# Scaled states ahead of the squares on ScalarE, the next unit's products behind the states on VectorE, and four weight halves made a unit earlier

## The chip, the cores and the metric

One core of one Trainium2 chip runs the whole program. The metric is the device time of one execution in microseconds; a change is compared by medians of several executions on the same chip.

## What is computed

Two batches of 768 tokens, 8 heads of 48. A recurrent attention with a decay per channel feeds a gated two-matrix layer, and that feeds a spatial gating layer:

```python
for t in range(S):
    cur = einsum('bhd,bhe->bhde', u * k[t], v[t])
    y[t] = einsum('bhd,bhde->bhe', r[t], state + cur)
    state = w[t][..., None] * state + einsum('bhd,bhe->bhde', k[t], v[t])
...
k = maximum(xk @ w_k, 0);  v = (k * k) @ w_v          # 384 -> 1024 -> 384
r = sigmoid(xr @ w_r);     x = r * v                  # 384 -> 384
...
h = gelu(x @ w_in);  u, v = halves of h               # 384 -> 1024
out = x + (u * (w_sg @ norm(v) + b_sg)) @ w_out
```

## The kernel before

The 1536 tokens are cut into four groups of 384 (three chunks of 128). The attention goes by **units**: a unit is one pair of heads in one group, so there are 16, numbered 0 to 15 here (the words "units 9 to 16" of the change are units 8 to 15). TensorE's order is written out by hand as a list of keys: for a unit S (transposes `kt_ps`, the bonus sum `ab`, the scores `sc`), K (the states `kv`), Y (masked scores times v into `y`) and Z (running states times `rp` into `y`), and for a group's first layer `k`, `r` and `v` (`moe1_k`, `moe1_r`, `moe1_v`). The units of group s+1 are spread between the matmuls of group s: units 8 to 11 lie in group 1's `k`, `r` and `v` (84 to 122 us), units 12 to 15 in group 2's (130 to 167 us). From there on TensorE runs the remaining layers without attention.

From group 1 on the `k` and `r` matmuls take each operand in two halves (high and low), three matmuls per product. The low halves are VectorE subtractions: `xkl`, `xrl` of the activations, `wkl`, `wrl`, `wvl` of the weights (`split1`, line 354; the high half `wh` is a ScalarE copy), `kl` of the squared k tile.

What a unit asks of the other engines, in the order of the data:

- `attn_prep` (line 444): VectorE scans `pf` and `pr` of the decays, then `kp` = k times `pr` and `rp` = r times `pf`.
- `rk_make` (line 477): GpSimd makes `ru` = r times k of the next unit, released by VectorE's `ru` product of this one; `bonus_halves` (line 531): ScalarE's `rh` high half and VectorE's `rh` low half of it, which TensorE's two `ab` matmuls read.
- `self_am` (line 540): VectorE masks the scores (`am`, two instructions), which Y reads.
- `attn_kv` (line 553): ScalarE's copy `kt` feeds the `kv` matmuls; VectorE turns them into running states (`zt`, and `zcar` for the group's last); ScalarE scales each into `sblk` or `scar`, two 48x48 instructions a state (line 592), which Z reads.
- `moe1_k` and `moe1_sq` (lines 742 and 755): for each of the eight k tiles ScalarE takes the relu `kr` out of PSUM, squares it into `kh` and then into `kr` itself, and VectorE subtracts them into `kl`. `kr` has two buffers, `mm` in PSUM has three.

On ScalarE and VectorE a scheduler sorts the instructions by a due time (`with at(t)`) where their data allow it; `tc.issue_after(x)` forbids an instruction to be put ahead of x on its engine. It adds order, not a transfer of data. DMAs on SP (SyncE) are sorted the same way. In the kernel before, a k tile's `kl` was held behind the unit's last state, and its squares were held by nothing:

```python
if split_ops[0] and s and (head.get("unit") or 0) > NP and (s, f) not in hold_sq:
    head.setdefault("kl", []).append(low)      # low: the subtraction alone
...
if kd == "K":
    for f in head.pop("kl", []):
        with tc.issue_after(st[g]["zt"]):
            f()
```

The eight `wkl` were made as five behind group 0's last `v` tile (`LO_HEAD = 5`, in `moe1_v`) and three later, from the list `lows`, which `LO_AT` empties behind the states of units 8, 9 and 10 (three, three and four halves).

Of the kernel before, what the change touches and what calls it, by code (L numbers as in the profile page):

```python
# [6 lines left out]
F32 = mybir.dt.float32  # L7
# [37 lines left out]
B_AM = 2  # L45
B_KP = 3
T_START = 7
LO_AT = {8: 3, 9: 3, 10: 4}
LO_LAST = 11
LO_HEAD = 5  # L50
T_GAP = 2.5
T_TAIL = 9.0
VQ = 4
# [19 lines left out]
def emit(tc, tin, nin, vt, consts, ucp, pars, b_sg, w_k, w_v, w_r, w_in, w_sgT, w_out, outT):  # L73
# [479 lines left out]
    def attn_kv(i):  # L553
        tY = TS["Y", i] if i < NP else TS["K", i] + 1.1
        s = st[i]
        hp = i % NP
        g, c0, nc_ = subs[i // NP]
        si = i // NP
        last = g % GB == GB - 1 and c0 + nc_ == CG
        nk = nc_ - 1 if last else nc_  # L560
        kv = pq.tile([128, 512], F32, name="kv", tag="kv", bufs=1)
        kv3 = kv[0:PR, 0:nc_ * D].rearrange("p (c d) -> p c d", d=D)
        for c in range(nk):
            for h in range(2):
                hs = slice(h * HP, HP if h == 0 else PR)
                PE.matmul(kv3[hs, c], s["kt"][:, c, hs], uv[i][:, c, h * D:h * D + D], start=(c == 0), stop=(c == nk - 1),
                          skip_group_check=True)
        zt = pa.tile([PR, max(1, nc_), D], F32, name="zt", tag="zt", bufs=2)
        first = g % GB == 0 and c0 == 0
        us = [None if first else scar[hp]]  # L570
        z = None if first else (zcar[:, (si + 1) % 2, hp, 0:D], zcar[:, (si + 1) % 2, hp, D:D + 1])
        for c in range(nk):
            o = zcar[:, si % 2, hp, 0:D] if c == nc_ - 1 else zt[:, c]
            with at(tY - 0.6 + (3 if c == nc_ - 1 else 0.2 * c)):
                if z is None:
                    s["zt"] = V.tensor_copy(o, kv3[:, c]).ins  # L576
                else:
                    s["zt"] = V.scalar_tensor_tensor(o, z[0], z[1], kv3[:, c], ALU.mult, ALU.add).ins
            z = (o, s["pe"][c])
            sb = scar[hp] if c == nc_ - 1 else sblk[i % 2][c]  # L580

            def scaled(c=c, o=o, sb=sb):
                if c == nc_ - 1:
                    with at(tY + 3):
                        A.activation(zcar[:, si % 2, hp, D:D + 1], s["pe"][c], AF.Copy)
                with at(tY - 0.5 + (3 if c == nc_ - 1 else 0.2 * c)):
                    for h in range(2):
                        hs = slice(h * HP, h * HP + D)
                        if i == NP - 1 and c == nc_ - 2:
                            V.tensor_scalar(sb[hs, hs], o[hs], s["pe"][c][hs], None, ALU.mult)  # L590
                        else:
                            s["sa"] = A.activation(sb[hs, hs], o[hs], AF.Copy, scale=s["pe"][c][hs]).ins  # L592

            if i < NP:
                s.setdefault("late" if c == nc_ - 1 else "soon", []).append(scaled)
            else:
                scaled()
            us.append(sb)
        s["us"] = us
# [142 lines left out]
    def moe1_k(s, f, c=None):  # L742
        nat, nt = is_nat(s, "k"), subs[s][2] * CH
        ps = moe1_part(s, "k", f, c)
        if ps is None:
            return
        kr = pl["w"].tile([128, nt], F32, name="kr", tag="kr", bufs=2)
        with at(TE["k", s, f]):
            m1[s, "ev", f] = A.activation(kr, ps, AF.Relu).ins
        if split_ops[0] and (s, f) in hold_sq:  # L750
            head["sq"] = lambda: moe1_sq(s, f, kr)
        else:
            moe1_sq(s, f, kr)

    def moe1_sq(s, f, kr):
# [13 lines left out]
        with at(dl):  # L769
            A.activation(kh, kr, AF.Square)  # L770
            A.activation(kr, kr, AF.Square)  # L771

        def low():
            with at(dl):
                V.tensor_tensor(kl, kr, kh.bitcast(F32), ALU.subtract)  # L775

        m1[s, "k", f] = (kh, kl)
        if split_ops[0] and s and (head.get("unit") or 0) > NP and (s, f) not in hold_sq:
            head.setdefault("kl", []).append(low)
        else:  # L780
            low()

    def moe1_r(s, j, c=None):
        nt = subs[s][2] * CH
# [8 lines left out]
    def moe1_v(s, j, q):  # L793
# [10 lines left out]
            V.tensor_tensor(x2[g][:, j, c0 * CH:(c0 + n) * CH], ps, m1[s, "r", j], ALU.mult)  # L804
        if s == NAT["r"] - 1 and j == KM - 1 and split_ops[0]:
            with tc.issue_after(st[2 * NP - 1]["ev"]), tc.issue_after(st[2 * NP - 1]["sa"]):
                for f in range(KF):
                    head["khi"] = split1("k", f, TS["k", s + 1, f], V, f >= LO_HEAD)

    m2 = {}  # L810

# [260 lines left out]
    for n, key in enumerate(keys[:n_in]):  # L1072
# [48 lines left out]
        if kd == "K" and 2 * NP <= g and g + 1 < NU and g != 3 * NP - 1:  # L1121
            with tc.issue_after(st[g]["zt"]):
                products(g + 1)
        if kd == "K" and g == 2 * NP:
            split_rv()
        if kd == "K" and g in LO_AT:
# [39 lines left out]
                    head.pop("sq")()  # L1166
        if kd == "K":
            head["unit"] = None
            for f in head.pop("kl", []):
                with tc.issue_after(st[g]["zt"]):  # L1170
                    f()
        if kd == "k" and key[2:] in ((0 if g in (0, NS - 1) else KM - 1,), (0 if g in (0, NS - 1) else KM - 1, KM - 1)) and g != 1:
            moe1_prep(g, 1, [] if g in (0, NS - 1) else [(m1[g, "ev", f],) for f in range(KM)])
        if kd == "v" and g == NS - 2 and key[2:] == (KM - 1, VQ - 1):
# [87 lines left out]
```

## Time and profile before

| | us |
|---|---|
| median of 3 executions | 338.54 (338.32 to 338.86) |
| the profiled execution | 338.41 |
| its span in the profile | 336.6 |
| TensorE busy in it | 326.6 |
| VectorE busy | 239.7 |
| ScalarE busy | 189.1 |
| GpSimd busy | 36.4 |

The profiled execution's own time is 1.8 us over its span, and 0.13 us under the median. Busy time on TensorE is from the start of a matmul to its modelled end, and neighbouring matmuls overlap, so a stretch in which TensorE waits briefly still reads as busy; the waits have to be read from start times. On VectorE and ScalarE too an instruction's length overlaps the next one's start by some 0.1 us where the two do not depend on each other.

### The profile page before, as it was taken

Reading aid. Unit: us, or ns where it says so; the run is one execution under the profiler, and the core shown is the slowest. Engines: PE = TensorE matmul, PEld = TensorE weight load, DVE = VectorE, ACT = ScalarE, POOL = GpSimd, SP = SyncE. Lnnn points to the kernel's source line nnn. Section 1 sums busy time; section 2 is a strip of 40 time slices with the busy share of each in tenths; the row PEclk is TensorE's granted clock in tenths of the full one; section 3 lists DMA queues with packets and bytes.
Section 4 is the critical chain, followed back from the end, with each engine's and each line's share of the span. In section 5 each row is a group of like instructions: output and inputs, shape, how many; then the busy total and the mean of one; then the engine's idle time right before and its main releaser. Section 6 shows DMA issues by size and latency. Waiting matters only on the chain.

```text
span 336.6 us, 5952 instructions
## 1 busy us (share of the span) xinstructions
PE 326.6 (97%) x2139; PEld 286.6 (85%) x2139; DVE 239.7 (71%) x537; ACT 189.1 (56%) x447; POOL 36.4 (11%) x60
## 2 busy tenths in 40 slices
PE   7999999999998999999999999999999999999993
PEld 3785666666897899988999999988999999999992
DVE  6988988678798996988559461797989723545531
ACT  3667995669977645986449973965533215211100
POOL 3210102010111101011022531000000000000000
PEclk9999999999999999999999999999999999999997
DMA  8888963755333423011026225413230010100022
GB/s 218 207 278 298 306 182 82 200 129 132 129 89 87 116 69 125 18 39 35 19 66 193 88 70 168 133 42 84 61 94 10 1 70 2 48 24 0 0 75 78
DMA packets 23878, 34.22 MB, mean 102 GB/s; under 512 B 3440, under 2 KB 18160, under 8 KB 23840
## 3 DMA queue, kind: packets, MB, share of 16 engines
q1 hardware_dynamic: 21696, 31.34, 32.0%
q10 hardware_dynamic: 2144, 2.41, 2.7%
q8 instruction: 19, 0.31, 0.4%
q14 instruction: 19, 0.16, 0.1%
HBM read 29.02 MB, written 2.36 MB: 93 GB/s over the span
## 4 chain that ended last, share of the span: by engine, by line
PE 65%; DVE 11%; issue 11%; DMA 5%; ACT 4%; POOL 2%; SPq 1%; POOLq 0%; ACTq 0%; DVEq 0%
PE mn L671 28%; PE mm L671 27%; DMA stg<-w_v 2%; DVE pf L458 2%; POOL ru L480 2%; PE y L624 2%; PE sc L514 2%; PE y L610 2%; DMA cst<-consts 2%; PE y L613 1%; DVE kl L775 1%; DVE pr L463 1%; DVE am L546 1%; DVE wvl L368 1%; PE mm L690 1%
## 5 line engine op out<-in xcount | busy, mean ns | idle before, releaser
L659 ACT ACTIVATE gah<-gt 128x384 fp32r<-128x384 f32 x16 | 8.4, 526 | 43.8 <-DVE gt L875 43.8
L480 POOL TENSOR_TENSOR ru<-urk 112x384 f32<-112x384 f32 x15 | 16.9, 1125 | 113.1 <-DVE ru L517 66.0
L592 ACT ACTIVATE sblk<-zt,pf 48x48 f32<-48x48 f32 x62 | 20.4, 330 | 7.1 <-DVE zt L576 3.9
L671 PE MATMUL mm<-kh,wh 128*128 128x384 f32 x64 | 22.0, 343 | 0.0
L671 PE MATMUL mm<-kh,wvl 128*128 128x384 f32 x64 | 21.6, 337 | 0.0
L671 PE MATMUL mm<-kl,wh 128*128 128x384 f32 x64 | 21.5, 336 | 0.0
L775 DVE TENSOR_TENSOR kl<-kr,kh 128x384 fp32r<-128x384 f32 x24 | 14.4, 601 | 9.1 <-ACT kr L771 9.1
L671 PE MATMUL mm<-xkh,wh 128*128 128x384 f32 x57 | 20.5, 360 | 0.0
L671 PE MATMUL mn<-wsh,vl 128*128 128x384 f32 x60 | 20.0, 334 | 0.0
L671 PE MATMUL mn<-wsh,vh 128*128 128x384 f32 x60 | 20.0, 334 | 0.0
L671 PE MATMUL mn<-wsl,vh 128*128 128x384 f32 x60 | 20.0, 334 | 0.0
L671 PE MATMUL mm<-xkh,wkl 128*128 128x384 f32 x57 | 19.2, 337 | 0.0
L671 PE MATMUL mm<-xkl,wh 128*128 128x384 f32 x57 | 19.2, 337 | 0.0
L546 DVE TENSOR_TENSOR am<-sc,cst 128x384 f32<-128x384 f32 x32 | 16.2, 547 | 1.3 <-PE sc L514 1.3
L671 PE MATMUL mm<-xkh,wk 128*128 128x384 f32 x48 | 17.0, 497 | 0.0
L458 DVE TENSOR_TENSOR_SCAN pf<-uw,d1f 112x387 f32<-112x387 f32 x16 | 15.3, 956 | 2.2 <-DMA uw<-tin 2.2
L334 POOL TENSOR_TENSOR w2l<-wf,w2h 128x384 fp32r<-128x384 f32 x12 | 12.9, 1091 | 35.4 <-ACT w2h L333 35.4
L671 PE MATMUL mm<-kh,wv 128*128 128x384 f32 x48 | 16.3, 490 | 0.0
L463 DVE TENSOR_TENSOR_SCAN pr<-uw,d1r 112x387 f32<-112x387 f32 x16 | 15.4, 960 | 0.2
L705 ACT ACTIVATE dx<-xx,par 128x384 f32<-128x384 f32 x22 | 12.9, 608 | 4.7 <-DMA xx<-yo 4.0
L514 PE MATMUL sc<-rp,kp 48*128 48x128 f32 x192 | 15.0, 289 | 0.0
L707 DVE SCALAR_TENSOR_TENSOR dx<-xx,par,dx 128x384 f32<-128x384 f32 x18 | 10.7, 610 | 5.6 <-ACT dx L705 5.6
(223 smaller groups left out, 978.5 us busy)
## 6 DMA issues: line engine op xcount, KB each, us to landing
urk<-tin SPq DMA_DIRECT2D x26, 144.0 KB, 3.1
wh<-w_k SPq DMA_DIRECT2D x8, 384.0 KB, 5.1
stg<-w_in SPq DMA_DIRECT2D x8, 384.0 KB, 3.7
wq<-tin SPq DMA_DIRECT2D x16, 168.0 KB, 2.4
wsf<-w_sgT SPq DMA_DIRECT2D x12, 192.0 KB, 4.7
outT<-ot SPq DMA_DIRECT2D x12, 192.0 KB, 1.9
uv<-nin ACTq DMA_DIRECT2D x14, 144.0 KB, 3.5
uw<-tin SPq DMA_DIRECT2D x26, 72.8 KB, 2.8
```

What stands on the lines that cost most here:

```text
L334: e.tensor_tensor(lo, full, hi.bitcast(F32), ALU.subtract)
L458: V.tensor_tensor_scan(pf[:, 0:n1], w[:, 0:n1], d1f[:, 0:n1], 1.0, ALU.mult, ALU.max)
L463: V.tensor_tensor_scan(pr[:, 1:wl][:, ::-1], w[:, 1:wl][:, ::-1], dr[:, 1:wl][:, ::-1], 0.0, ALU.mult, ALU.add)
L480: return e.tensor_tensor(rks[i], urk[i][:, 0], urk[i][:, 1], ALU.mult).ins
L514: PE.matmul(sc[h][:, c], s["kp"][hs, c], s["rp"][hs, c], start=True, stop=True)
L546: s["am"] = V.tensor_tensor(am[:, h], sc[h], mask, ALU.mult).ins
L592: s["sa"] = A.activation(sb[hs, hs], o[hs], AF.Copy, scale=s["pe"][c][hs]).ins
L659: A.activation(hi, src, AF.Copy)
L671: PE.matmul(ps, l, r, start=(first and k == 0), stop=(last and k == len(prods) - 1))
L705: ins = [A.activation(d, xj[:, 1 + t0:1 + t1], AF.Copy, scale=mu[:, j:j + 1]).ins]
L707: V.scalar_tensor_tensor(ops[0][:, j] if nat else d, xj[:, t0:t1], nu[:, j:j + 1], d, ALU.mult, ALU.add)
L775: V.tensor_tensor(kl, kr, kh.bitcast(F32), ALU.subtract)
```

## The change

1. A k tile whose matmuls end inside a unit (group 1 and later) no longer has its two squares issued with its relu: `moe1_sq` as a whole (squares and subtraction) is kept in `head["kl"]`.
2. After the unit's K key these run behind two instructions: the next unit's `rp` (`st[g + 1]["last"][1]`) and this unit's last `sblk` scaling (`st[g]["sb"]`, new).
3. Four `wkl` (tiles 0 to 3, `LO_EARLY = 4`) are split behind unit 6's states and scalings; the other four stay where they were, none is put off to `lows`, and `LO_AT` takes two, two and three.

```diff
-LO_AT = {8: 3, 9: 3, 10: 4}
+LO_AT = {8: 2, 9: 2, 10: 3}
-LO_HEAD = 5
+LO_EARLY = 4
...
                             s["sa"] = A.activation(sb[hs, hs], o[hs], AF.Copy, scale=s["pe"][c][hs]).ins
+                            if c < nc_ - 1:
+                                s["sb"] = s["sa"]
...
         if split_ops[0] and (s, f) in hold_sq:
             head["sq"] = lambda: moe1_sq(s, f, kr)
+        elif split_ops[0] and s and (head.get("unit") or 0) > NP:
+            head.setdefault("kl", []).append(lambda: moe1_sq(s, f, kr))
         else:
             moe1_sq(s, f, kr)
...
             A.activation(kr, kr, AF.Square)
-
-        def low():
-            with at(dl):
-                V.tensor_tensor(kl, kr, kh.bitcast(F32), ALU.subtract)
-
+            V.tensor_tensor(kl, kr, kh.bitcast(F32), ALU.subtract)
         m1[s, "k", f] = (kh, kl)
-        if split_ops[0] and s and (head.get("unit") or 0) > NP and (s, f) not in hold_sq:
-            head.setdefault("kl", []).append(low)
-        else:
-            low()
...
-                for f in range(KF):
-                    head["khi"] = split1("k", f, TS["k", s + 1, f], V, f >= LO_HEAD)
+                for f in range(LO_EARLY, KF):
+                    head["khi"] = split1("k", f, TS["k", s + 1, f], V)
...
+        if kd == "K":
+            for f in head.pop("kl", []):
+                with tc.issue_after(st[g + 1]["last"][1] if g + 1 in st else st[g]["zt"]), tc.issue_after(st[g]["sb"]):
+                    f()
+        if kd == "K" and g == 2 * NP - 2:
+            with tc.issue_after(st[g]["zt"]), tc.issue_after(st[g]["sa"]):
+                for f in range(LO_EARLY):
+                    split1("k", f, TS["k", 1, f] - 12, V)
...
         if kd == "K":
             head["unit"] = None
-            for f in head.pop("kl", []):
-                with tc.issue_after(st[g]["zt"]):
-                    f()
```

TensorE's and GpSimd's orders are the same in both kernels. Three places of the others, word for word, before and then after.

ScalarE in unit 9, from the high half `rh` for unit 10 to the scaling into `scar1` (names end in a buffer number; `kr_1279` and `kr_1295` before are `kr_1283` and `kr_1295` after, the k tiles 4 and 5 of group 1). Before:

```order
L535 ACTIVATE rh_1374<-ru_1270,cst_70 112x384
L749 ACTIVATE kr_1279<-mm_1216 128x384
L770 ACTIVATE kh_1281<-kr_1279 128x384
L771 ACTIVATE kr_1279<-kr_1279 128x384
L749 ACTIVATE kr_1295<-mm_1285 128x384
L770 ACTIVATE kh_1297<-kr_1295 128x384
L592 ACTIVATE sblk10_88<-zt_1307,pf_997 48x48 x2
L592 ACTIVATE sblk11_89<-zt_1307,pf_997 48x48 x2
L771 ACTIVATE kr_1295<-kr_1295 128x384
L592 ACTIVATE scar1_83<-zcar_81,pf_997 48x48 x2
```

After:

```order
L535 ACTIVATE rh_1376<-ru_1274,cst_70 112x384
L751 ACTIVATE kr_1283<-mm_1220 128x384
L751 ACTIVATE kr_1295<-mm_1285 128x384
L592 ACTIVATE sblk10_88<-zt_1304,pf_1011 48x48 x2
L592 ACTIVATE sblk11_89<-zt_1304,pf_1011 48x48 x2
L774 ACTIVATE kh_1317<-kr_1283 128x384
L774 ACTIVATE kh_1322<-kr_1295 128x384
L775 ACTIVATE kr_1283<-kr_1283 128x384
L775 ACTIVATE kr_1295<-kr_1295 128x384
L592 ACTIVATE scar1_83<-zcar_81,pf_1011 48x48 x2
```

Three squares that stood ahead of the four `sblk` scalings stand behind them, and the second tile's relu stands next to the first's.

VectorE from behind unit 9's states (`zcar`) to the first mask of unit 10. Before:

```order
L775 TENSOR_TENSOR kl_1282<-kr_1279,kh_1281 128x384
L467 TENSOR_TENSOR kp_1239<-urk1_109,pr_1237 112x384
L470 TENSOR_TENSOR rp_1238<-urk1_109,pf_1236 112x384
L775 TENSOR_TENSOR kl_1282<-kr_1295,kh_1297 128x384
L537 SCALAR_TENSOR_TENSOR rh_1375<-ru_1270,cst_70,rh_1374 112x384
L368 TENSOR_TENSOR wrl_1320<-wr_610,wh_1172 128x384
L458 SCALAR_TENSOR_TENSOR pf_1367<-uw2_107,d1f_72 112x387
L634 TENSOR_TENSOR yo_1356<-y_1328,ru_1121 112x384
L517 TENSOR_TENSOR ru_1270<-ab_1387,uvt_111 112x384
L460 RECIPROCAL d1r_90<-pf_1367 112x3
L368 TENSOR_TENSOR wrl_1322<-wr_615,wh_1172 128x384
L546 TENSOR_TENSOR am_1384<-sc_1385,cst_70 128x384
```

After:

```order
L467 TENSOR_TENSOR kp_1243<-urk1_109,pr_1241 112x384
L470 TENSOR_TENSOR rp_1242<-urk1_109,pf_1240 112x384
L537 SCALAR_TENSOR_TENSOR rh_1377<-ru_1274,cst_70,rh_1376 112x384
L458 SCALAR_TENSOR_TENSOR pf_1369<-uw2_107,d1f_72 112x387
L776 TENSOR_TENSOR kl_1318<-kr_1283,kh_1317 128x384
L776 TENSOR_TENSOR kl_1318<-kr_1295,kh_1322 128x384
L460 RECIPROCAL d1r_90<-pf_1369 112x3
L368 TENSOR_TENSOR wrl_1326<-wr_620,wh_1183 128x384
L636 TENSOR_TENSOR yo_1358<-y_1330,ru_1127 112x384
L517 TENSOR_TENSOR ru_1274<-ab_1389,uvt_111 112x384
L463 SCALAR_TENSOR_TENSOR pr_1370<-uw2_107,d1r_90 112x387
L546 TENSOR_TENSOR am_1386<-sc_1387,cst_70 128x384
```

`kp`, `rp` and `rh` come first and the two `kl` after the scan `pf`; one weight half fewer stands in the stretch, and the scan `pr`, which before came behind the masks, now stands ahead of them.

VectorE around unit 7's masks, where the four early weight halves are put. Before:

```order
L460 RECIPROCAL d1r_90<-pf_915 112x3
L634 TENSOR_TENSOR yo_904<-y_885,ru_754 112x384
L463 SCALAR_TENSOR_TENSOR pr_916<-uw2_107,d1r_90 112x387
L517 TENSOR_TENSOR ru_857<-ab_935,uvt_111 112x384
L546 TENSOR_TENSOR am_932<-sc_933,cst_70 128x384
```

After (two more `wkl` stand just ahead of `yo`):

```order
L368 TENSOR_TENSOR wkl_890<-wk_496,wh_885 128x384
L636 TENSOR_TENSOR yo_918<-y_899,ru_754 112x384
L517 TENSOR_TENSOR ru_857<-ab_949,uvt_111 112x384
L368 TENSOR_TENSOR wkl_894<-wk_507,wh_892 128x384
L546 TENSOR_TENSOR am_946<-sc_947,cst_70 128x384
```

The two scans of unit 8, with their reciprocal, move from ahead of unit 7's masks to behind them, and weight halves take their place. On SP one thing moves: the reload of `uw` for unit 12 stands ahead of the three `w_in` loads instead of behind them.

## Rows read from the trace of the kernel before

**Rows 1.** The page, part 1: busy us, share of the span and count by engine.
```profile
PE 326.6 (97%) x2139; PEld 286.6 (85%) x2139; DVE 239.7 (71%) x537; ACT 189.1 (56%) x447; POOL 36.4 (11%) x60
```

**Rows 2.** Busy time by unit (8, 9, 10, 12, 13, 14): stretch, length, engines, clock, DMA.
```profile
86.52:94.72 8.20, 8.20 (x74) 7.39 (x73) 5.20 (x13) 7.84 (x20) 1.02 (x1) 1.00 0.20 48
94.72:103.41 8.69, 8.46 (x74) 7.45 (x73) 7.88 (x18) 6.38 (x16) 1.32 (x1) 1.00 0.34 95
103.41:112.53 9.12, 8.19 (x71) 6.98 (x70) 8.82 (x20) 6.69 (x18) 1.33 (x1) 1.00 0.39 97
...
132.34:140.65 8.31, 8.31 (x72) 7.50 (x71) 7.63 (x15) 7.51 (x19) 1.01 (x1) 1.00 0.08 21
140.65:149.47 8.82, 8.63 (x72) 7.61 (x71) 7.57 (x17) 6.89 (x17) 1.26 (x1) 1.00 0.13 35
149.47:158.48 9.01, 8.75 (x69) 7.32 (x68) 7.39 (x15) 5.85 (x15) 1.00 (x1) 1.00 0.14 35
```

**Rows 3.** The chain that ended last, behind unit 15: start, us, what.
```profile
167.49 8.41 PE mm L671 x48
```

**Rows 4.** TensorE's timeline, units 8 to 10: start, us, instructions, [idle before <-releaser].
```profile
90.42 0.49 PE L566 MATMUL kv<-uv,kt 128*64 128x48 f32 x11
...
102.49 0.39 PE L624 MATMUL y<-rp,sblk 112*112 112x128 f32 x2
103.11 0.47 PE L624 MATMUL y<-rp,sblk 112*112 112x128 f32 x2 [0.23 <-ACT sblk L592]
...
104.78 0.43 PE L510 MATMUL ab<-rh,hblk 112*112 112x384 f32 x1 [0.74 <-DVE rh L537]
...
108.68 0.83 PE L610 MATMUL y<-am,uv 128*64 128x128 f32 x11
```

**Rows 5.** TensorE's timeline, unit 14.
```profile
153.77 1.32 PE L610 MATMUL y<-am,uv 128*64 128x128 f32 x12
```

**Rows 6.** Waits from 62 to 166 us: engine and line, releaser, total, times, longest.
```profile
DVE kl L775 <- ACT kr L771: 4.4, 5, 1.3
```

**Rows 7.** ScalarE's timeline, unit 9.
```profile
99.26 0.47 ACT L749 ACTIVATE kr<-mm 128x384 f32<-128x384 f32 x1
...
100.75 0.47 ACT L749 ACTIVATE kr<-mm 128x384 f32<-128x384 f32 x1
101.25 0.53 ACT L770 ACTIVATE kh<-kr 128x384 fp32r<-128x384 f32 x1
101.69 1.37 ACT L592 ACTIVATE sblk<-zt,pf 48x48 f32<-48x48 f32 x4
```

**Rows 8.** VectorE's timeline, from unit 8's last state to unit 10's masks.
```profile
91.56 0.27 DVE L578 SCALAR_TENSOR_TENSOR zcar<-zt,pf,kv 112x48 f32<-112x48 f32 x1
...
93.95 0.56 DVE L775 TENSOR_TENSOR kl<-kr,kh 128x384 fp32r<-128x384 f32 x1 [0.71 <-ACT kr L771]
...
97.74 1.02 DVE L546 TENSOR_TENSOR am<-sc,cst 128x384 f32<-128x384 f32 x2
...
99.14 0.96 DVE L463 TENSOR_TENSOR_SCAN pr<-uw,d1r 112x387 f32<-112x387 f32 x1
...
101.00 0.27 DVE L578 SCALAR_TENSOR_TENSOR zcar<-zt,pf,kv 112x48 f32<-112x48 f32 x1
...
103.64 0.56 DVE L775 TENSOR_TENSOR kl<-kr,kh 128x384 fp32r<-128x384 f32 x1 [0.96 <-ACT kr L771]
...
107.42 1.02 DVE L546 TENSOR_TENSOR am<-sc,cst 128x384 f32<-128x384 f32 x2
```

**Rows 9.** GpSimd's and VectorE's timelines where the two meet.
```profile
56.79 1.53 POOL L480 TENSOR_TENSOR ru<-urk 112x384 f32<-112x384 f32 x1 [5.76 <-DVE ru L517]
134.13 1.11 DVE L711 TENSOR_TENSOR xrl<-dx,xrh 128x384 fp32r<-128x384 f32 x1 [0.40 <-ACT xrh L710]
```

**Rows 10.** SP's timeline ahead of unit 8, and DMA issues of 70 to 92 us to landing.
```profile
81.38 1.38 SPq L316 DMA_DIRECT2D stg<-w_in  x3
...
stg<-w_in SPq DMA_DIRECT2D x3, 384.0 KB, 4.3
```

## The prediction, before the changed kernel had run

> **What bounds the kernel.** I read the busy shares first: TensorE 97%, VectorE 71%, ScalarE 56% [rows 1]. The end is set by TensorE's own order, so the change can only give what TensorE loses by waiting. Busy time hides short waits, so next I cut the time by unit, from one unit's transposes to the next's [rows 2]. The reader should compare lengths and counts: unit 8 takes 8.20 us, unit 9 with the same matmuls 8.69; unit 10 has three matmuls fewer and takes 9.12. A matmul costs 8.41 / 48 = 0.175 us in the dense stretch behind the units [rows 3], so three are 0.53. Units 9 and 10 are thus 0.49 and 9.12 - (8.20 - 0.53) = 1.45 over unit 8. Group 2's units have one state fewer and a carry more; by unit 12 (8.31), unit 13 is 0.51 over and unit 14, again three matmuls short, 9.01 - (8.31 - 0.53) = 1.23. Sum: **3.68 us** in four units. The clock column is 1.00 in all of them, full speed, so this is waiting and not a slower matmul. Unit 11 shows no wait and behind unit 15 the matmuls are dense.
>
> Then TensorE's timeline, for what each wait ends on. In unit 9 the second pair of Z matmuls starts 0.62 behind the first and ends a wait on `sblk`; right behind it unit 10's second `ab` matmul waits 0.74 on `rh` [rows 4]. Unit 10's 1.45 is 0.99 of this `ab` wait (its transposes have begun by then) and 0.45 of its own `sblk` wait. In unit 14, `y` takes 1.32 [rows 5], where unit 10's takes 0.83 [rows 4]: it starts before its masks are done; the rest of that unit's excess, about 0.6, is again Z.
>
> Last, the two engines that are waited for. On ScalarE in unit 9 the relu of tile 4 starts at 99.26, its two squares follow, then tile 5's relu at 100.75 and first square at 101.25, and only then the scalings, 101.69 to 103.06 [rows 7]. VectorE had the states done earlier: `zcar`, the last, started at 101.00 [rows 8]. On VectorE `kl` waits 0.71 and 0.96 for a ScalarE square [rows 8], 4.4 us in five places [rows 6], and `rh`, which TensorE wants, is queued behind it.
>
> **The change, part by part.** *Scalings ahead of squares.* Unit 9's `sblk` loses tile 4's two squares (1.0 us, from 99.26 + 0.5 to 100.75) and tile 5's first (0.44). With both relus done by 100.2 the states decide: even unmoved ones, done at 101.2, give scalings done by 101.2 + 1.37 = 102.57 at worst, and Z's second pair wants the last at 102.49 + 0.22 = 102.71. With the states earlier (below), the margin is over a microsecond. In units 10, 13 and 14 the same pieces go, 1.0 to 1.4 us before waits of 0.43 to 0.6. Removed: 0.49 (unit 9), 0.45 (10), 0.41 (13), 0.60 (14).
>
> *Next `kp`, `rp`, `rh` behind the states.* A VectorE product of this size is 0.55 long, 0.47 from start to start where nothing waits. In unit 9 `rh` now comes two of these behind `zcar`, done near 102.8 instead of 104.7; TensorE comes to the second `ab` 0.9 behind Z's first matmul, at 103.4. Removed: 0.99.
>
> *Masks.* Here the order could take something back. From `zcar` to the masks is 101.00 to 107.42 = 6.42 [rows 8]. New: less the wait of 0.96, less one weight half (0.47), plus the scan `pr`, now ahead of the masks (0.96 long, 0.87 from start to start): 5.86. In unit 8 to 9 likewise 97.74 - 91.56 = 6.18 becomes 6.18 - 0.71 - 0.47 + 0.87 = 5.87; and from the masks to the next `zcar`, 101.00 - 97.74 = 3.26, the scan leaves: 2.39. So unit 9's states are 0.31 + 0.87 = 1.18 earlier and unit 10's masks 1.18 + 0.56 = 1.74 earlier. TensorE reaches unit 10's `y` 0.49 + 0.99 = 1.48 earlier than 108.68, at 107.2 [rows 4]; the masks would end at 108.44 - 1.74 = 106.7. Margin 0.5, if the two `kl` now put in front do not wait. They may: squares end 4 x 0.34 + 4 x 0.44 = 3.1 behind the first scaling, and VectorE arrives after `kp`, `rp`, `rh`, `pf`, 2.35 behind a state end that lies 0.5 behind the first state. That is a draw, with 0.1 to 0.3 of waiting to be expected. From state to state in units 9 and 10 VectorE needs 5.87 + 2.39 = 8.26 and 8.25 against TensorE's 8.20 and 7.67; the 0.6 too much comes out of the distance between states and Z (over 2 us), not out of TensorE. In unit 13 VectorE gains nothing before the masks, and I leave 0.10 of its 0.51 for them. In unit 14 the masks were late by the `kl` waits in front; without these 0.63 goes.
>
> *Held squares.* `kr` has two buffers and `mm` three. A relu two tiles on must now wait for a later `kl`. In unit 9 the bank that tile 7 needs is freed by tile 4's relu, done at 99.26 + 0.47 [rows 7], some 1.5 us before TensorE begins tile 7. That relu follows `rh`, as before, and needs a `kl` made a unit earlier. I price this at nothing; if the relu came over 1.5 us later, TensorE would wait for the bank.
>
> *Four weight halves earlier.* Four copies (as long as a square, 0.44) on ScalarE and four subtractions on VectorE go to unit 7. Ahead of its masks stand three of these, 1.41, in place of two scans and a reciprocal, 0.87 + 0.87 + 0.1 = 1.84, which are unit 8's and wanted only some 15 us later. Unit 7's masks thus come 0.4 earlier: no cost. What is freed is the weight half counted above.
>
> *SP.* The `w_in` loads, issued from 81.38 on [rows 10], now stand behind a reload that waits for unit 9's scan `pr`, in my order done at about 82.4: about 2 us later. ScalarE has two casts of these tiles ahead of unit 8's `kt`; landing took 4.3 us [rows 10], so the casts end near 89, `kt` near 89.4, and the `kv` matmuls want it at 90.42 [rows 4]. Cost: zero with 1 us of cover; without cover at most 1 us.
>
> **Sum.** 3.68 less the 0.10 that stays, less 0.2 for the draws at `kl` (between 0 and 0.5): 3.4 us. 338.41 - 3.4 = **335.0 us**; the profiled execution that this starts from is 0.13 below the median. Behind unit 15 everything hangs on TensorE's, VectorE's and ScalarE's own order, so the gain should pass to the end whole. 0.2% is 0.7 us, about what a measurement of this kernel can tell from no change.
>
> **Rivals.**
>
> *VectorE binds the units (0.15).* In units 9 and 10 it is busy 7.88 of 8.69 and 8.82 of 9.12 [rows 2]. If it were the limit, order would give nothing and only work taken out would: three of the four halves, 3 x 0.47 = 1.4 us, and group 2 would keep its waits: 337.0. For it: the 8.26 above. Against it: 4.4 us that VectorE itself stands waiting for squares [rows 6]. The Trainium skill, Perfetto Trace Analysis, section Identifying the Most-Contended Engine, says that occupancy is for VectorE a fair measure of how close it is to its limit, and that the engine with the most should be optimized first. By that rule this rival, 337.0, would be the likely one; the rows with the waits speak for 335.0.
>
> *Scan against GpSimd (0.06).* The scan `pr` is put right behind `ru`, just when GpSimd starts the next `ru`. The two do not run together: `ru` took 1.53 beside a scan that had begun, and a VectorE subtraction took 1.11, twice its usual 0.55, where GpSimd was first [rows 9]. I expect the scan first: it can start 0.46 after `ru`'s start, and GpSimd must see `ru` end. Then the next `rh` half is 0.2 later than beside the masks, covered. If GpSimd is first, the masks of units 9 and 10 lose about 1.0 each, 0.5 over their margin: 336.0. The Trainium skill, GPSIMD Engine Reference, section Key points, says that GpSimd shares its SBUF interfaces with VectorE and contends with VectorE instructions that have two SBUF inputs, which both do here; it does not say who goes first.
>
> *ScalarE parked behind `w_in` (0.06).* If those loads land 2 us later than my estimate, unit 8's `kt` is late by 1: 336.0.
>
> *Waits change places (0.07).* Z no longer waits, `y` does, for as much: 338.4. For it: the draw at `kl`. Against it: the margin of 0.5 at unit 10.
>
> *Slower (0.06).* VectorE now stands in order behind two squares that stand behind four scalings. If ScalarE gets to the scalings late (it must first make `rh`, which waits for GpSimd), the squares, both `kl` and then `ru`, scan and masks are late, and `y` waits in every unit. If `kl` waits 0.9 in units 8 to 10 and 12 to 14, six times, that is 5.4 against 3.6 gained: 340.2. It decides for slower from 0.6 a unit plus the margin.
>
> That the change does not do what it says is out: the orders of both engines show it.
>
> **Numbers.** My forecast has 0.60 (334.5 to 335.7; the low end is all of 3.68 and 0.2 of small delays besides). Faster by over 0.2%: 0.60 + 0.15 + 0.06 + 0.06 = 0.87; within: 0.07; slower: 0.06. The range 334.5 to 337.2 takes in the three partial cases and leaves out the last two.
>
> **What would show it.** Right: units 9 and 10 near 8.2 and 7.7 long, 13 and 14 near 8.4 and 7.8; no `sblk` or `rh` wait on TensorE; scalings directly behind two relus; `kl` waits on VectorE well below 4.4. VectorE binding: the same lengths as before with `y` held by masks. Scan: a `pr` near 1.5 long. Parked ScalarE: a wait of `kv` on `kt` at 90. Wrong altogether: TensorE waiting for `mm` banks, or unit 8 longer than 8.2.

## The result, and the profile after

The changed kernel takes **335.3 us** (334.82 to 335.46, four runs) where the kernel before takes 338.5 (338.32 to 338.86, four runs): ratio 0.9902, 95% interval 0.9885 to 0.9919. A second measurement, on another occasion, gave 335.28 and 0.9898 (0.9883 to 0.9913). Forecast was 335.0, with 334.5 to 335.7 as its own range. The profiled execution took 335.18, its span is 333.3.

The busy shares (page, part 1) hardly moved [rows 1]; TensorE's busy time fell by 1.1 us:

```profile
PE 325.5 (98%) x2139; PEld 286.2 (86%) x2139; DVE 239.5 (72%) x537; ACT 187.1 (56%) x447; POOL 37.3 (11%) x60
```

The lengths by unit (busy time by stretch, units 8, 9, 10, 12, 13, 14; columns as in [rows 2]) say where it went:

```profile
86.99:95.18 8.19, 8.19 (x73) 7.38 (x72) 5.76 (x13) 7.46 (x19) 1.02 (x1) 1.00 0.37 122
95.18:103.39 8.21, 8.21 (x75) 7.41 (x74) 8.14 (x19) 6.73 (x18) 1.60 (x1) 1.00 0.43 110
103.39:111.08 7.69, 7.69 (x72) 6.88 (x70) 7.42 (x18) 6.18 (x18) 1.60 (x1) 1.00 0.36 93
130.83:139.14 8.31, 8.31 (x71) 7.50 (x70) 7.65 (x15) 7.17 (x18) 1.01 (x1) 1.00 0.08 21
139.14:147.46 8.32, 8.32 (x72) 7.51 (x71) 8.18 (x19) 6.85 (x18) 1.26 (x1) 1.00 0.15 39
147.46:155.24 7.78, 7.78 (x70) 6.98 (x69) 6.44 (x14) 5.91 (x16) 1.02 (x1) 1.00 0.15 38
```

Units 9, 10, 13 and 14 became shorter by 0.48, 1.43, 0.50 and 1.23: 3.64 us of the 3.68 that the prediction counted. TensorE's timeline shows no wait at the places of [rows 4]; the four Z matmuls are one dense piece, the second `ab` is 0.24 behind the first (1.15 before):

```profile
102.95 0.60 PE L626 MATMUL y<-rp,sblk 112*112 112x128 f32 x4
...
103.61 0.41 PE L509 MATMUL ab<-rh,hblk 112*112 112x384 f32 x1
103.85 0.34 PE L510 MATMUL ab<-rh,hblk 112*112 112x384 f32 x1
...
107.61 0.28 PE L612 MATMUL y<-am,uv 128*48 128x128 f32 x1
```

ScalarE's timeline of unit 9 has the scalings right behind two relus, 1.7 us earlier than in [rows 7], and the squares behind them:

```profile
98.74 0.62 ACT L535 ACTIVATE rh<-ru,cst 112x384 fp32r<-112x384 f32 x1 [1.35 <-POOL ru L480]
99.26 0.85 ACT L751 ACTIVATE kr<-mm 128x384 f32<-128x384 f32 x2
100.00 1.38 ACT L592 ACTIVATE sblk<-zt,pf 48x48 f32<-48x48 f32 x4
101.40 0.94 ACT L774 ACTIVATE kh<-kr 128x384 fp32r<-128x384 f32 x2
102.25 0.92 ACT L775 ACTIVATE kr<-kr 128x384 f32<-128x384 f32 x2
```

VectorE's timeline from unit 8's last state to unit 10's masks, to be read against [rows 8]: `rh` comes 1.1 behind the states (3.1 before, 101.00 to 104.11) and no `kl` waits in this stretch.

```profile
92.03 0.26 DVE L578 SCALAR_TENSOR_TENSOR zcar<-zt,pf,kv 112x48 f32<-112x48 f32 x1
...
96.94 0.96 DVE L463 TENSOR_TENSOR_SCAN pr<-uw,d1r 112x387 f32<-112x387 f32 x1
97.81 1.00 DVE L546 TENSOR_TENSOR am<-sc,cst 128x384 f32<-128x384 f32 x2
...
100.21 0.27 DVE L578 SCALAR_TENSOR_TENSOR zcar<-zt,pf,kv 112x48 f32<-112x48 f32 x1
...
101.33 0.61 DVE L537 SCALAR_TENSOR_TENSOR rh<-ru,cst,rh 112x384 fp32r<-112x384 f32 x1
...
102.79 1.03 DVE L776 TENSOR_TENSOR kl<-kr,kh 128x384 fp32r<-128x384 f32 x2
...
106.07 0.99 DVE L546 TENSOR_TENSOR am<-sc,cst 128x384 f32<-128x384 f32 x2
```

In the waits from 62 to 166 us, the 4.4 us of [rows 6] have become

```profile
DVE kl L776 <- ACT kr L775: 0.8, 2, 0.6
```

The span fell by 3.3 us, not by 3.64, since this execution came to unit 8 0.47 us later (86.99 against 86.52). At unit 5's transposes 0.41 of it was there already (45.39 against 44.98), 20 us ahead of the first instruction that the change moves, so that part is the spread of executions and not the change. Over the fourteen profiles, one for each run, TensorE reaches unit 7 between 65.92 and 66.77 us; the two of the changed kernel have 66.36 and 66.74. The last 0.05 arises between units 7 and 8, where the two kernels differ; more on this stretch below.

### The profile page after: what moved, and what is told of

It reads as the page before. It is cut to its first block, busy times and chain, and to the rows that moved or that the text cites. A ratio compares the mean times of both kernels' runs of the same rounds, so it can differ in the third digit from the quotient of the medians.

```text
span 333.3 us, 5954 instructions
## 1 busy us (share of the span) xinstructions
PE 325.5 (98%) x2139; PEld 286.2 (86%) x2139; DVE 239.5 (72%) x537; ACT 187.1 (56%) x447; POOL 37.3 (11%) x60
## 4 chain that ended last, share of the span: by engine, by line
PE 90%; ACT 3%; DMA 3%; DVE 1%; issue 1%; SPq 1%; ACTq 0%; DVEq 0%
PE mm L673 46%; PE mn L673 28%; PE sc L514 4%; PE y L612 3%; PE y L626 3%; PE kv L566 2%; DMA cst<-consts 2%; DMA wh<-w_r 1%; PE kt_ps L490 1%; ACT top L327 1%; PE y L615 1%; PE mm L495 1%; ACT sblk L592 1%; DVE pf L458 1%; PE ab L509 1%
## 5 line engine op out<-in xcount | busy, mean ns | idle before, releaser
L458 DVE TENSOR_TENSOR_SCAN pf<-uw,d1f 112x387 f32<-112x387 f32 x16 | 16.0, 1005 | 2.4 <-DMA uw<-tin 2.4
L327 ACT ACTIVATE top<-stg 128x384 f16<-128x384 bf16 x17 | 10.9, 642 | 8.4 <-DMA stg<-w_in 3.1
```

The lines of the kernel that those rows point to most:

```text
L327: A.activation(box(top.bitcast(F16).rearrange("p (f w) -> p f w", w=2)[:, :, 1]), end, AF.Copy)
L458: V.tensor_tensor_scan(pf[:, 0:n1], w[:, 0:n1], d1f[:, 0:n1], 1.0, ALU.mult, ALU.max)
```

## The experiments

The theory was that TensorE's four units lose 3.68 us to the order of ScalarE and VectorE, and that VectorE's load is no bound. The rival was the load: three weight halves fewer would then be the gain. Later runs took the change apart by engine, measured VectorE's room, and tried the explanation that came out of them.

### Halves alone, and order alone

The first kernel is the one before with the early halves only (`LO_AT`, `LO_EARLY` and the block behind unit 6); the second is the changed one without them.

```diff
 (second kernel, against the changed one)
-LO_AT = {8: 2, 9: 2, 10: 3}
+LO_AT = {8: 3, 9: 3, 10: 4}
...
-                for f in range(LO_EARLY):
-                    split1("k", f, TS["k", 1, f] - 12, V)
```

Expected of the halves alone: 

> The kernel before with one part of the change alone: the four k weight halves made in unit 7, so that units 8, 9 and 10 each carry one weight half fewer on VectorE; the squares, kl and the products keep their old order. Theory (the units lost time to order, not to VectorE's load): ScalarE's squares still stand ahead of the scalings and rh still behind kl, whose waits only grow by what VectorE saves; 338.2 us, between 338.0 and 338.6, and the sblk and rh waits of units 9 and 10 stay within 0.3 of before. Rival (VectorE's load binds units 8 to 10): three halves of 0.47 come out of the time, 337.1 us.

Expected of the order alone: 

> The changed kernel without the early halves: the squares behind the scalings, kl behind kp, rp and rh, but units 8, 9 and 10 carry their old number of weight halves; the scan pr then stands behind the masks again in this order. Theory (order is all of the gain): the masks of units 9 and 10 have a margin of 0.55 us before y, two halves more and a scan moved take at most 0.1 of it; 335.4 us, between 335.2 and 335.9. Rival (VectorE's load binds): three halves of 0.47 come back, 336.7 us.

Halves alone: **339.62 us** against 338.79, ratio 1.0024 (1.0015 to 1.0033), slower. The load rival falls, but so does my number. Most of the loss is in unit 9 (9.27 us long, 8.69 before), and the timelines of ScalarE, VectorE and TensorE show it come through: SP issues `w_in` from 84.06 us on, where [rows 10] has 81.38, ScalarE stands waiting for it ahead of unit 8's squares, `kl` waits 1.26, `rh` is late for TensorE.

```profile
87.41 0.64 ACT L327 ACTIVATE top<-stg 128x384 f16<-128x384 bf16 x1 [2.29 <-DMA stg<-w_in]
```
```profile
95.06 0.56 DVE L775 TENSOR_TENSOR kl<-kr,kh 128x384 fp32r<-128x384 f32 x1 [1.26 <-ACT kr L771]
```
```profile
96.20 0.43 PE L510 MATMUL ab<-rh,hblk 112*112 112x384 f32 x1 [0.33 <-DVE rh L537]
```

Order alone: **336.25 us**, 0.9926 (0.9913 to 0.9939). It brings three quarters of the gain, and 0.8 us less than I said. Units 9, 13 and 14 are as in the changed kernel; units 10 and 11 are not (7.69 and 19.75 there):

```profile
102.95:111.07 8.12, 8.12 (x72) 7.11 (x71) 7.89 (x18) 6.06 (x17) 1.31 (x1) 1.00 0.43 107
111.07:131.46 20.39, 20.16 (x140) 18.94 (x139) 18.11 (x38) 10.27 (x24) 1.36 (x2) 1.00 0.41 112
```

With `pr` (0.87) behind the masks, the last state starts 3.26 us behind them, 2.40 in the changed kernel, and the scalings wait for the states, as VectorE's and ScalarE's timelines of the order-alone kernel show:

```profile
97.35 1.02 DVE L546 TENSOR_TENSOR am<-sc,cst 128x384 f32<-128x384 f32 x2
...
100.61 0.27 DVE L578 SCALAR_TENSOR_TENSOR zcar<-zt,pf,kv 112x48 f32<-112x48 f32 x1
```

```profile
100.31 1.39 ACT L592 ACTIVATE sblk<-zt,pf 48x48 f32<-48x48 f32 x4 [0.59 <-DVE zt L576]
```

In unit 11 Z waits for `sblk` again. Units 10 and 11 lose 0.43 and 0.64 us in this way, and the stretch ahead of unit 8 is 0.25 shorter than in the changed kernel (20.38 against 20.63). So the early halves are worth 0.8 to 0.9 us in the new order (0.9926 against 0.9902 and 0.9898); whether by the lighter VectorE or by the scan's place, which changes with it, no run separates. In the old order they brought nothing that this pair shows.

### The late `w_in`, put right

Unit 9's scan `pr` is held behind the mixing of inputs (the `dx` and `xkl` instructions on VectorE), so SP issues `w_in` ahead of the reload that waits for this scan, as before the change.

```diff
         next(head["prep", i])
-        next(head["prep", i])
+        if i != 2 * NP + 1:
+            next(head["prep", i])
...
+                    with tc.issue_after(v):
+                        next(head["prep", g + 2])
```

Halves alone with this: 

> The early halves alone, as before, but with unit 9's scan pr held behind the mixing of its inputs, so that the three w_in loads stand in SP's queue ahead of the reload that waits for that scan, as in the kernel before. Theory (the early halves alone cost 0.8 us because w_in came 2 us later, ScalarE stood 2.3 us waiting for it in unit 8, and kl, rh and the masks of unit 9 came 1.1 late): no such wait, unit 9 back to 8.7, ratio to the kernel before 0.998 to 1.0005, 338.5 us where before is 338.8. Rival (the early halves cost in another way, for instance by what they put ahead of unit 7): stays at 1.0024, 339.6.

The changed kernel with this: 

> The changed kernel with the same hold on unit 9's scan, so that w_in is ahead of the reload again. Theory (in the new order ScalarE's late start in unit 8 has only kl behind it, which nothing hurries): ScalarE's 2.3 us wait goes, VectorE's kl wait of 0.57 in unit 8 goes, TensorE had no wait there, so the time is that of the changed kernel within 0.2%. Rival (the late w_in still costs the changed kernel what it costs the early halves alone): 0.8 us faster, 334.6.

The changed kernel beside them: 

> The changed kernel itself, beside the three below on the same chip, as their yardstick. Its ratio to the kernel before should be 0.990 again (0.9885 to 0.9919); its TensorE should reach unit 8 anywhere from 86.5 to 87.1 us if the 0.47 us that the first profile lost ahead of unit 7 is spread from execution to execution, and again near 87.0 if it belongs to the change.

Halves alone: 338.54 against 338.56, ratio 1.0002 (0.9993 to 1.0011); units 9 and 10 are 8.70 and 9.12, as before. So the hold takes the 0.8 us back, and the halves by themselves give nothing. But the hold does two things, and the 0.8 has two parts. Unit 9 went from 9.27 to 8.70, 0.57, which is the late `w_in`. The other 0.24 lies between units 7 and 8, before ScalarE reads `w_in`. Without the hold unit 9's scan `pr` runs at 82.09, ahead of the mixing; `xkl` then starts at 84.94 (84.22 with the hold, and there the scan follows), and TensorE's weight load (PEld) waits for it. That wait in the list of the halves alone, and the stretch from unit 7 to unit 8 without and with the hold:

```profile
PEld mm L671 <- DVE xkl L711: 0.3, 1, 0.3
```
```profile
66.42:87.05 20.63, 20.63 (x104) 13.66 (x103) 18.79 (x38) 14.52 (x35) 1.25 (x1) 1.00 0.47 124
```
```profile
66.01:86.40 20.39, 20.39 (x105) 13.68 (x103) 18.80 (x38) 15.43 (x38) 1.25 (x1) 1.00 0.52 153
```

Changed kernel: **335.03**, 0.9896 (0.9881 to 0.9911), beside 335.28 without. ScalarE's waits for the tiles are down from 2.32 to 0.92 and 0.49, `kl` of unit 8 no longer waits (0.57 before) and TensorE's units 8 to 14 are the same to 0.01, so the late `w_in` costs the changed kernel nothing there. The stretch from unit 7 to unit 8, though, is again 0.24 shorter with the hold:

```profile
66.36:86.99 20.63, 20.63 (x104) 13.64 (x103) 18.78 (x38) 14.46 (x35) 1.25 (x1) 1.00 0.50 128
```
```profile
66.09:86.48 20.39, 20.39 (x104) 13.68 (x103) 18.90 (x38) 14.94 (x37) 1.25 (x1) 1.00 0.51 149
```

The medians differ by as much, 0.25, but with four executions each (335.14 to 335.77 and 334.61 to 335.45) they do not show by themselves that this version beats the changed kernel. The changed kernel beside them reached unit 8 at 87.37 us, outside the 86.5 to 87.1 that I expected; its lead-in was the later one of the two, by 0.38 at unit 7.

### VectorE's part alone, ScalarE's part alone

For VectorE's part the squares are issued with the relus again, and only `kl` is held, behind the next `rh`. For ScalarE's part the squares stay held, and the next `rh` is put behind both `kl`. Both keep the early halves, and `kp` and `rp` ahead of `kl`.

```diff
 (VectorE's part, against the changed kernel)
-        elif split_ops[0] and s and (head.get("unit") or 0) > NP:
-            head.setdefault("kl", []).append(lambda: moe1_sq(s, f, kr))
...
+        if kd == "S":
+            for f in head.pop("kl", []):
+                with tc.issue_after(st[g]["rl"]):
+                    f()
 (ScalarE's part, against the changed kernel)
-        with at(TS["S", i] - 2), tc.issue_after(st[i]["last"][0]), tc.issue_after(st[i]["last"][1]):
+        with at(TS["S", i] - 2), tc.issue_after(st[i]["last"][0]), tc.issue_after(st[i].get("kli", st[i]["last"][1])):
```

VectorE's part: 

> The changed kernel with ScalarE's squares back in their old place, ahead of the scalings, and only VectorE's part kept: both kl held until behind the next unit's kp, rp and rh. Theory: rh and mask waits stay away (0.99 and 0.63), the sblk waits come back where the chain on ScalarE starts no earlier than before, at least unit 13's 0.41, at most all four, 1.95; 336.0 us, between 335.7 and 337.3. Rival 1 (the scalings' place is the whole of it): 337.2 or more, with sblk waits of 0.4 to 0.6 in units 9, 10, 13 and 14. Rival 2 (the sblk waits only followed late states): no wait on sblk, 335.3.

ScalarE's part: 

> The changed kernel with ScalarE's part kept, the squares behind the scalings, and VectorE's undone: the next unit's rh stands behind both kl. Theory (the two parts need each other): no sblk waits, but kl now comes when the later squares are done, and rh behind it reaches TensorE 0.5 to 1.4 us late in each of six units; 339 us, between 337.8 and 340.5, with waits of the ab matmuls on rh. Rival (the scalings carry the gain, and rh gives back only the 0.99 it cost before): 336.3.

VectorE's part with `w_in` first: 

> VectorE's part alone, as before (kl behind the next rh, squares ahead of the scalings), with w_in first as in the run that undid the early halves' cost. Theory (of that run's 1.74 us of lost time in units 9 and 10 the late start of ScalarE in unit 8 made the first half; the loop from masks to masks, 9.1 us with kl still behind a square that stands behind the scalings, makes the second): unit 9 back to 8.2, unit 10 still 8.5, group 2 as before; 0.85 us faster than without, 337.8, between 337.4 and 338.2 where before is 338.6. Rival (VectorE's part gives nothing by itself): 338.6.

The same again: 

> The same kernel as the run before last (VectorE's part alone, w_in first) again, for a second profile: in the first one w_in's second tile landed 6 us after its issue, ScalarE read it at 88.2, and that execution took 338.66 us, while four others of the same program took 337.4 to 337.8. Theory (the late landing is the whole difference): an execution in which the tile is read near 86.5 has unit 9 at 8.2 to 8.3 us and unit 10 at 8.5 to 8.7, and takes 337.6. Rival (the profile shows what the program always does): unit 9 at 9.1 again.

VectorE's part: **338.75**, 1.0000 (0.9991 to 1.0009). My 336.0 was far off. No `ab` matmul waits for `rh` any more, but `kl` still waits, 4.4 us in all as in [rows 6], and all four `sblk` waits are there, those of units 9 and 10 larger than before (the units are 9.06 and 8.58 long). With `w_in` first it takes 337.70, 0.9965 (0.9952 to 0.9979), and 337.21, 0.9961 (0.9947 to 0.9975), in the second measurement (337.8 and 337.6 were expected). The profile of the first shows units as long as without (9.08 and 8.59). That execution is the slowest of its five, 338.66 against 337.38 to 337.77; in it `w_in` was issued 0.5 to 0.8 us later than in the other profiles with this hold and landed 1.5 to 2.0 us later. ScalarE's two casts of it, in the first profile and in the second:

```profile
86.25 0.65 ACT L327 ACTIVATE top<-stg 128x384 f16<-128x384 bf16 x1 [1.31 <-DMA stg<-w_in]
88.23 0.65 ACT L327 ACTIVATE top<-stg 128x384 f16<-128x384 bf16 x1 [1.33 <-DMA stg<-w_in]
```
```profile
85.46 0.65 ACT L327 ACTIVATE top<-stg 128x384 f16<-128x384 bf16 x1 [0.77 <-DMA stg<-w_in]
86.70 0.64 ACT L327 ACTIVATE top<-stg 128x384 f16<-128x384 bf16 x1 [0.58 <-DMA stg<-w_in]
```

Units 9 and 10 of the second (by stretch):

```profile
94.52:102.72 8.20, 8.20 (x75) 7.40 (x73) 7.42 (x17) 6.31 (x16) 1.33 (x1) 1.00 0.37 102
102.72:111.28 8.56, 8.33 (x72) 7.05 (x71) 8.30 (x19) 6.66 (x18) 1.32 (x1) 1.00 0.34 84
```

That is the 8.2 and 8.5 expected. VectorE's part, rid of the late `w_in`, is worth 1.05 us in group 1 (8.69 + 9.12 - 8.20 - 8.56) and nothing in group 2 (units 13 and 14: 8.83 and 9.00).

ScalarE's part: **340.15**, 1.0054 (1.0038 to 1.0070), slower. No `sblk` wait is left, but TensorE waits for `rh` six times; the waits list and the worst one, in unit 13:

```profile
PE ab L510 <- DVE rh L537: 3.1, 6, 1.3
```
```profile
142.37 0.43 PE L510 MATMUL ab<-rh,hblk 112*112 112x384 f32 x1 [1.29 <-DVE rh L537]
```

`w_in` is as late here (2.69 us of wait on ScalarE), and the `kl` at 90.37 waits 0.94 behind it, but the two from 94.27 on, which `rh` follows, don't wait. By the ratios, one half of the change gives nothing, or 1.2 to 1.3 us with `w_in` first, the other costs 1.8, and together they give 3.3.

### VectorE's room

One mask product more in units 8 to 10 and 12 to 14 (the second half written twice).

```diff
                 s["am"] = V.tensor_tensor(am[:, h], sc[h], mask, ALU.mult).ins
+                if h and i in (8, 9, 10, 12, 13, 14):
+                    with tc.issue_after(s["am"]):
+                        s["am"] = V.tensor_tensor(am[:, h], sc[h], mask, ALU.mult).ins
```

> The changed kernel with one mask product more (0.46 us from start to start, the second half written twice) in units 8 to 10 and 12 to 14, to see how much room VectorE has left. From the changed kernel's trace the masks end 0.56, 0.55, 0.28, 0.06 and 0.6 us before y in units 9, 10, 12, 13 and 14. Theory (VectorE is full now, its margin is what the trace shows): group 1 loses 0.4, group 2 loses 0.9, in all 1.2 us more than the changed kernel, between 0.7 and 1.7. Rival 1 (TensorE is the bound with a microsecond of cover): no change. Rival 2 (VectorE is the bound outright): six times 0.46, 2.8 us.

**337.46 us**, 0.9964 (0.9952 to 0.9976): 2.2 us over the changed kernel, beyond my range and short of the second rival's 2.8. `y` waits for masks in units 9, 10, 12 and 13 (0.35, 0.71, 0.32 and 0.70 longer, 2.1 in all), not in unit 14. TensorE's timeline in unit 10:

```profile
108.57 0.40 PE L615 MATMUL y<-am,uv 128*64 128x128 f32 x2
109.26 0.85 PE L615 MATMUL y<-am,uv 128*48 128x128 f32 x10 [0.30 <-DVE am L549]
```

My estimate left out that in units 9 and 10 the scheduler puts a weight half ahead of the third mask, and in unit 13 the scan `pr`, so `y` waits for two instructions and not for one. The room in group 1 is some 0.5 us, as read, and less in units 12 and 13; six products of 0.46, 2.8 us, cost 2.2.

### Weight halves taken out of the loop

By now the pace of units 9 and 10 looked like a loop over three engines (described below, under what the prediction lacked). On the kernel with the early halves and `w_in` first, in the old order, the two halves left in each of units 8 to 10 are held behind the masks:

```diff
-        if kd == "K" and g in LO_AT:
-            split_lo(LO_AT[g], st[g]["zt"])
...
+            if g in (2 * NP + 1, 2 * NP + 2):
+                with tc.issue_after(st[g]["am"]):
+                    next(head["prep", g + 1])
+            if g - 1 in LO_AT:
+                split_lo(LO_AT[g - 1], st[g]["am"])
```

> The kernel of the run with early halves and w_in first (old order of squares, kl and products; level with before), and beside that the two weight halves left in each of units 8 to 10 held behind the masks, and pr kept behind them too. Theory (a loop sets the pace of units 9 and 10: masks, GpSimd's ru and ScalarE's rh, relus, squares and scalings, kl, rh, the next masks, 9.68 us in the trace of before against TensorE's 8.2; a half counts only where it stands in the loop, between kl and the masks): two halves leave the loop, 0.94 each time; the sblk waits of units 9 and 10 go, the rh wait shrinks little, since rp now stands behind kl; 337.5 us, between 337.0 and 337.9, where before is 338.5. Rival (only the place of the squares counts): level with before.

**338.78**, 1.0001 (0.9990 to 1.0013): level with before, the rival's number. The stretches of units 9, 10 and 11 say that both are at work:

```profile
95.05:103.25 8.20, 8.20 (x74) 7.46 (x73) 7.07 (x17) 6.49 (x17) 1.01 (x1) 1.00 0.36 98
103.25:112.15 8.90, 7.94 (x71) 6.96 (x70) 8.83 (x20) 6.76 (x18) 1.02 (x1) 1.00 0.39 100
112.15:132.53 20.38, 20.09 (x140) 18.96 (x139) 17.25 (x36) 9.21 (x21) 2.67 (x2) 1.00 0.41 112
```

Units 9 and 10 are 0.72 shorter than with the halves in front (8.70 and 9.12), with the squares where they were: both `sblk` waits are gone, the `rh` wait stays, 0.96. That the `sblk` waits go was expected, and the rival excludes it; the gain is short of the 1.0 expected. Unit 11 gives 0.6 back (19.75 to 20.38): seven `wvl` halves now stand behind its masks, and a matmul there waits for one. I had not counted that.

### One group only

Units 12 to 14 in the old order, units 8 to 10 as changed.

```diff
-        elif split_ops[0] and s and (head.get("unit") or 0) > NP:
+        elif split_ops[0] and s and NP < (head.get("unit") or 0) < 3 * NP:
...
+            for f in head.pop("kl2", []):
+                with tc.issue_after(st[g]["zt"]):
+                    f()
```

> The changed kernel with squares, kl and products of units 12 to 14 back in the old order, units 8 to 10 as changed. Theory (the groups do not depend on each other): units 9 and 10 stay at 8.2 and 7.7, units 13 and 14 lose their 0.51 and 1.23 again; 1.7 us over the changed kernel, 337.0, between 336.6 and 337.3. Rival (what the changed order gains in group 1 is met by later waits of group 2 whatever its order): other than 1.7 by over 0.5.

**336.91**, 0.9944 (0.9930 to 0.9957), 1.6 us over the changed kernel by the medians of two occasions, 1.4 to 1.6 by the ratios: units 9 and 10 at 8.20 and 7.70, units 13 and 14 at 8.84 and 9.01. The two groups add up.

## Why the prediction was right, point by point

**The sum.** It was read from unit lengths, and 3.64 of 3.68 went. The 0.10 left to unit 13 and the 0.2 for draws at `kl` were not lost on TensorE. So the sum should have been 338.41 - 3.64 = 334.8, and 0.3 was taken off it for losses that did not come. The profiled execution took 335.18, mainly because it came to unit 8 0.47 us later, which no term of the prediction has. That the two nearly cancel, and the number is met to 0.2 (0.3 by the median), is luck; the lengths of the units are not.

**VectorE's course.** From states to masks 5.87 and 5.86 were forecast; measured 5.78 and 5.86. From masks to states 2.39; measured 2.40. Margin of unit 10's masks before `y` 0.5; measured 107.61 - 107.06 = 0.55. The two `kl` ahead of unit 10's masks do not wait, where 0.1 to 0.3 was forecast; the `kl` waits that are left are 0.57 in unit 8, the late `w_in`, and 0.20 behind unit 10's states.

**Four weight halves earlier, "no cost"; SP, "cost 0".** `kt` was done at 89.28, forecast 89.4, and TensorE asked at 90.89. Right for units 8 to 14 of the changed kernel. But the price belongs to the order it stands in: in the old one the same late `w_in` costs 0.57 us in unit 9, since `rh` stands behind `kl`. And one cost of 0.24 was not seen: the halves bring unit 9's scan ahead of the mixing, and TensorE waits for `xkl` ahead of unit 8. It does not show in the sum, since the kernel before lost 0.19 in the same stretch (20.58 long, 20.63 after, 20.39 with the hold).

**Held squares, priced at nothing.** Right: ScalarE's relus wait for a `kl` once, 0.3 us, and TensorE waits for no bank.

**The scan and GpSimd.** The scan went first and kept its length, 0.96 at 96.94. GpSimd's timeline has `ru` at the 1.5 of [rows 9]:

```profile
97.10 1.60 POOL L480 TENSOR_TENSOR ru<-urk 112x384 f32<-112x384 f32 x1 [7.61 <-DVE ru L517]
```

In the run with the halves behind the masks `pr` is not at that place, and the same `ru` (97.28) takes 1.01, beside the masks' PSUM reads. The Trainium skill, GPSIMD Engine Reference, section Key points, says that GpSimd shares its SBUF interfaces with VectorE and contends with VectorE instructions that have two SBUF inputs; these lengths agree, 1.60 beside a scan with two of them and 1.01 beside masks that read one operand from PSUM.

**The rivals.** "VectorE binds" (337.0) missed the time, but holds in part: without the early halves the new order gives 2.5 of 3.3 us, and 0.5 us a unit more on VectorE costs 2.2. The Trainium skill (Perfetto Trace Analysis, section Identifying the Most-Contended Engine) says to optimize the engine with the highest occupancy first. In units 9 and 10 that is VectorE by [rows 2], 7.88 and 8.82 us, with TensorE judged by its weight loads (PEld), 7.45 and 6.98, as the section does. Here taking load alone gave 1.0002; it counted only once the order was mended. "Slower" would have been the outcome had `rh` stayed behind `kl`: ScalarE's part alone measured 340.15. That this is near the rival's 340.2 is chance. The rival has `kl` waiting 5.4 us for squares and `y` waiting for masks; here `kl` waits 1.1 in all and TensorE waits for `rh`, which is queued behind both `kl`.

**What the prediction lacked** is the link between its terms. It gave each wait to one move (scalings 1.95, `rh` 0.99, masks 0.63). The runs by engine show that these do not add: the waits are places where one loop meets TensorE. In [rows 7, 8] it goes from unit 9's masks (97.74) over GpSimd's `ru`, `rh`, relus and squares to the scalings (101.69), over the square behind them to the second `kl` (103.64), and over `rh`, scan, products and halves on VectorE to the next masks (107.42): 3.95 + 1.95 + 3.78 = 9.68 us, where TensorE needs 8.2. The masks only mark the place: GpSimd's `ru` does not wait for them but for VectorE's `ru` product ahead of them, and starts first, as its timeline before shows (the profile names the reciprocal `d1r`, which stands right behind that product and ends at 97.38):

```profile
97.38 1.32 POOL L480 TENSOR_TENSOR ru<-urk 112x384 f32<-112x384 f32 x1 [8.36 <-DVE d1r L460]
```

From one such product to the next it is 9.68 too (96.75 to 106.43). In the changed kernel it is masks 97.81, scalings 100.00, first `kl` 102.79, masks 106.07: 2.19 + 2.79 + 3.28 = 8.26. But there VectorE's timeline shows no wait on the way: from unit 8's last state to the end of the weight half behind unit 10's `rh` it is busy 18.47 of 18.62 us (busy time by stretch, third figure of the engines). So this 8.26 is VectorE's own work from masks to masks, as the prediction added it up from state to state.

```profile
92.03:110.65 18.62, 18.62 (x158) 17.01 (x158) 18.47 (x41) 15.57 (x43) 3.20 (x2) 1.00 0.37 96
```

With VectorE's part alone (second profile) it is 9.16, and unit 10 still 0.9 over:

```profile
97.02 1.01 DVE L546 TENSOR_TENSOR am<-sc,cst 128x384 f32<-128x384 f32 x2
...
106.18 1.01 DVE L546 TENSOR_TENSOR am<-sc,cst 128x384 f32<-128x384 f32 x2
```

In these runs a wait taken off one place of the loop turned up at its next, and that every leg was moved would be why the sum came true. The loop fits all runs of group 1, but as a mechanism it is argued more than shown. The one run that tested it directly, by taking two halves out, shortened it by 0.23, to 9.45, and not by the 0.94 expected; in it `rp` (0.47) had come to stand behind the second `kl`, inside the loop:

```profile
97.12 1.01 DVE L546 TENSOR_TENSOR am<-sc,cst 128x384 f32<-128x384 f32 x2
...
106.57 1.00 DVE L546 TENSOR_TENSOR am<-sc,cst 128x384 f32<-128x384 f32 x2
```

Its gain of 0.72 in units 9 and 10 was lost again in unit 11. Group 2 was not taken apart.

## What to carry to other kernels

Measure by stretches of equal work what an engine loses, and forecast the sum from that; do not share it out among moves by the name on each wait. Where two engines wait for each other once per round, write down the loop with its length beside the bound engine's round: moving one leg can give nothing, or cost, until the others are moved too. Load taken from an engine counted here only where it lay on that loop; in the changed kernel VectorE's waits in units 9 and 10 are gone, and the run with a mask product more suggests that its load is the next limit there.

## What the runs showed that I had not expected

A DMA's landing can go with a longer execution: where the three `w_in` loads were issued from 81.97 us on, the second of the two casts came at 88.23; in the four other profiles with the hold they were issued from 81.2 to 81.5 on, and it came at 86.3 to 86.7. In the kernel with VectorE's part alone the late execution took 338.66 us against 337.4 to 337.8 for its neighbours, and its unit 9 was 0.9 us longer than in the second profile (9.08 and 8.20). And executions of one program reach the same early point up to 0.4 us apart (66.36 and 66.74 at unit 7 for the changed kernel), more than the difference between several of the versions tried here: unit lengths told them apart where single times could not.
